# A fused attention and softplus-FFN kernel: loads of q and k in 1 KB packets, w_in in 2 KB packets, a load order planned per tensor, last blocks in free score banks

## Chip, cores, metric

The kernel runs on one core of a Trainium2 chip. The metric is the device time of one execution in microseconds; the profile's span (first to last instruction) is about 1.8 us shorter. Most executions of this kernel agree within about 1%; a run more than 1.5% above the fastest of its kernel counts as slow and is left out of every ratio.

PE is the matrix engine and PEld its weight loads, DVE the vector engine, ACT the scalar engine, POOL the general engine. SyncE (SP in the profile) and ACT issue the loads; SPq and ACTq are their issue queues. "First unit" means the first one or two attention blocks.

## The reference, cut to what matters

```python
# q, k, v: (4, 8, 768, 64) f32; n_global 8, n_local 96; w_in (512, 2048), w_out (2048, 512)
scores = q @ k.T / 8 + bias            # bias = -slope[head] * distance
keep   = (key < 8) | ((0 <= query - key) & (query - key < 96))
a      = softmax(where(keep, scores, -1e9))
x      = (a @ v) as (3072, 512)        # 24 blocks of 128 rows
h      = x @ w_in                      # "first layer"
out    = softplus(h) @ w_out           # "second layer"
```

## The kernel before

The Python file is a small scheduler. Every instruction is declared as an `op` with an engine, an estimated duration, a rank, and the tiles it reads and writes. A planner simulates the engines and the load queues at build time and writes the instructions out in that order. On the chip, each engine then works strictly through its own list.

The settings that the change touches:

```python
FIRST_UNITS = [[0], [1], [2, 3]]       # first block of sequence 0; of 1; of 2 and 3 together
FIRST_LOADS = "u0 u1 u2 i0 i1 i2 i3 i4 i5 i6 i7 o0 u3 o1 ...".split()
ACT_UNITS = 2                          # second halves of units 0 and 1 are issued by ACT
FILLERS = 90                           # idle matmuls that keep PE's clock up at the start
O_KEYS = {(0, 1): ("s", 3), (1, 0): ("s", 2)}   # where second-layer sums are kept; default "o"
```

Every load of a first unit is two halves (64 partitions each, 512-byte runs), the second half issued by ACT for units 0 and 1. w_in comes as eight loads of 256 columns (1 KB runs) behind all three units; POOL casts all of them to bf16.

```python
def load_unit(i, rank, second="SP"):
    for x, which in enumerate("qkv"):
        ... # later units: one 512 KB load
        for y in range(2):
            eng = second if y else "SP"
            def fn(...):
                return dma_on[eng].dma_start(
                    raw_t[slot][64 * y : 64 * y + 64, 0 : P * nh].rearrange("p (h c) -> p h c", h=nh),
                    part.rearrange("h (p r) d -> p h (r d)", r=2))
```

PSUM holds one score tile of four banks and four tiles of one bank each. The second layer accumulates 16 matmuls into `bank(key)`, and DVE copies the sum out.

```python
s_ps = ps.tile([P, 16, P], F32, name="s_ps")     # four banks, ONE tile
x_ps = ps.tile([P, 512], F32, name="x_ps"); o_ps = ps.tile([P, 512], F32, name="o_ps")
def bank(key):
    if key[0] == "s":
        return s_ps[:, 4 * key[1] : 4 * key[1] + 4, :].rearrange("p a b -> p (a b)")
    return {"x": x_ps, "o": o_ps, "h0": h_ps[0], "h1": h_ps[1]}[key[0]][:]
```

The biases of the later blocks (`dist`, `biasA`: two distance tiles and eight products) are built by DVE early and in its gaps: the distances by 5.7 us, five of the products by 11.6 us and the last three from 20.7 to 21.4 us.

The softmax here doesn't subtract the row's maximum and nothing guards it: scores larger than these inputs give would overflow.

## Time and profile before

| | before |
|---|---|
| time, median of 3 | 235.15 us (233.95 to 236.61) |
| span of the profiled run | 232.6 us |
| PE busy | 214.6 us, 92% |
| first first-layer matmul | 21.2 us |
| sixteen slots of eight first-layer matmuls: last weight load | 50.2 us |
| last weight load of the second layer | 228.2 us |

From the page of the kernel before: the span, and the rows by slices of 5.8 us (busy tenths of PE, granted clock in tenths, and GB/s moved by the DMA engines).

```profile
span 232.6 us, 5037 instructions
...
PE   8979889898995998999999999999999999999883
...
PEclk9999999999998899999999999999999999999998
...
GB/s 156 224 235 350 352 305 375 360 253 223 199 270 168 122 93 239 190 187 216 133 166 163 133 135 119 243 131 242 168 188 176 113 73 68 48 45 36 10 93 45
```

PE's row looks full from the start, but the first 20 us are mostly fillers. To see what is useful I counted PE's weight loads in the trace (one per matmul, and none is missing) and multiplied them by pitches read from the timeline: 0.109 us for a first-layer matmul, 0.2165 for a second-layer matmul or a bias seed, 0.03 to 0.055 for the small ones, nothing for a filler. Every kernel has 195.4 us of useful work by this count. "Lost" below means time minus useful work, and it can be read by stretch:

| kernel before | 0 to 60 us | 60 to 100 | 100 to 220 | 220 to end |
|---|---|---|---|---|
| lost, us | 22.9 | 6.6 | 1.9 | 5.9 |

So there are three places to gain: the start, 60 to 100 us, and the end. These windows of the kernel before show the busy time of each engine, the granted clock, the DMA share and GB/s:

```profile
5.00:10.00 5.00, 4.48 (x41) 3.60 (x40) 2.47 (x10) 2.97 (x10) 1.90 (x5) 1.00 1.03 237
10.00:15.00 5.00, 3.52 (x43) 2.48 (x40) 2.68 (x11) 1.85 (x3) 0.53 (x3) 1.00 1.21 220
15.00:20.00 5.00, 4.95 (x64) 4.20 (x65) 4.78 (x12) 1.08 (x2) 4.43 (x7) 1.00 1.12 304
...
60.00:100.00 40.00, 36.16 (x353) 24.46 (x357) 21.19 (x36) 28.81 (x36) 18.78 (x36) 0.96 0.79 187
```

The timelines of the kernel before, first ACT (its issue queue and its first exponential), then PE. Columns: start, duration, engine, line, operation, tiles, count, and in brackets the idle time before it and what ended it.

```profile
3.72 0.60 ACTq L323 DMA_DIRECT2D raw<-in_k_dram  x1
...
8.74 0.60 ACTq L323 DMA_DIRECT2D raw<-in_v_dram  x1
...
11.57 0.60 ACT L581 ACTIVATE pb<-s_ps 128x512 bf16<-128x512 f32 x1 [0.92 <-DVE biasA L793]
```

```profile
10.81 0.40 PE L546 MATMUL s_ps<-qT,kTf 64*128 64x128 bf16 x8
...
21.17 1.05 PE L657 MATMUL h_ps<-XT,w_in_bf 128*128 128x256 bf16 x8
...
220.75 3.61 PE L704 MATMUL o_ps<-w_out_bf,g 128*128 128x512 bf16 x16 [0.78 <-DVE osb L728]
225.15 3.61 PE L704 MATMUL o_ps<-w_out_bf,g 128*128 128x512 bf16 x16 [0.78 <-DVE osb L728]
```

The first scores stand at 10.8 us and the first layer starts at 21.2 us. At the end PE waits twice, 0.78 us each, until DVE has copied the previous block out of the one bank they share.

### The profile page before, as it was taken

How to read it: one execution, taken by the hardware profiler on the slowest of the kernel's cores; microseconds unless marked ns; L12 is line 12 of the kernel's file. 1: busy time of each engine (PE TensorE's matmuls, PEld its weight loads, DVE VectorE, ACT ScalarE, POOL GpSimd, SP SyncE). 2: the span in 40 equal slices, each digit the busy share in tenths (PEclk: the TensorE clock that was granted, in tenths of full speed). 3: DMA queues.
4: the chain of work that ended last, by engine and by line, in shares of the span. 5: the costliest groups of instructions: out<-in, count | busy, mean ns of one | idle time of the engine just before them, and what ended most of it. 6: DMA issues, size and time to landing. Idle time of an engine off the chain costs nothing.

```text
span 232.6 us, 5037 instructions
## 1 busy us (share of the span) xinstructions
PE 214.6 (92%) x1994; PEld 149.0 (64%) x2026; DVE 113.1 (49%) x219; ACT 154.9 (67%) x202; POOL 98.1 (42%) x178
## 2 busy tenths in 40 slices
PE   8979889898995998999999999999999999999883
PEld 5758777555753476777667667676766867667531
DVE  5567315474179494059538448732944862111111
ACT  2432977751985259898878959876885987676600
POOL 3437645789456224767701606341573630000000
PEclk9999999999998899999999999999999999999998
DMA  5999999999796449868877545899679422110021
GB/s 156 224 235 350 352 305 375 360 253 223 199 270 168 122 93 239 190 187 216 133 166 163 133 135 119 243 131 242 168 188 176 113 73 68 48 45 36 10 93 45
DMA packets 76872, 40.97 MB, mean 176 GB/s; under 512 B 30640, under 2 KB 71856, under 8 KB 76848
## 3 DMA queue, kind: packets, MB, share of 16 engines
q1 hardware_dynamic: 75216, 39.86, 68.2%
q10 hardware_dynamic: 1632, 0.79, 1.4%
q8 instruction: 16, 0.26, 0.5%
q14 instruction: 8, 0.07, 0.1%
HBM read 27.26 MB, written 6.29 MB: 144 GB/s over the span
## 4 chain that ended last, share of the span: by engine, by line
PE 78%; DMA 7%; DVE 4%; POOL 3%; issue 3%; ACT 3%; DVEq 0%; POOLq 0%; ACTq 0%
PE o_ps L704 30%; PE h_ps L657 29%; PE s_ps L546 5%; PE h_ps L807 5%; DMA raw<-in_k_dram 4%; PE s_ps L704 3%; DMA raw<-in_v_dram 3%; PE x_ps L601 2%; ACT pb L581 2%; PE x_ps L598 2%; DVE z L572 2%; POOL vb L501 2%; POOL vb L395 1%; DVE osb L728 1%; PE s_ps L443 1%
## 5 line engine op out<-in xcount | busy, mean ns | idle before, releaser
L657 PE MATMUL h_ps<-XT,w_in_bf 128*128 128x256 bf16 x768 | 95.5, 273 | 1.5 <-POOL w_in_bf L350 0.9
L704 PE MATMUL o_ps<-w_out_bf,g 128*128 128x512 bf16 x323 | 84.8, 385 | 4.0 <-DVE osb L728 1.6
L657 PEld LDWEIGHTS <-w_in_bf 128*128 128x128 bf16 x768 | 73.2, 98 | 20.2 <-POOL w_in_bf L350 2.2
L672 ACT ACTIVATE e<-h_ps 128x512 f32<-128x512 f32 x96 | 59.9, 630 | 30.9 <-PE h_ps L657 30.3
L704 PEld LDWEIGHTS <-g 128*128 128x128 bf16 x384 | 35.9, 99 | 36.2 <-issue 7.0
L572 DVE TENSOR_TENSOR z<-s_ps,biasA 128x1024 f32<-128x1024 f32 x40 | 48.1, 1218 | 18.7 <-PE s_ps L546 17.0
L581 ACT ACTIVATE pb<-z 128x1024 bf16<-128x1024 f32 x40 | 41.8, 1050 | 18.9 <-DVE z L572 18.8
L683 ACT ACTIVATE g<-e 128x1024 bf16<-128x1024 f32 x48 | 50.7, 1056 | 1.3
L395 POOL CAST vb<-raw 64x512 bf16<-64x512 f32 (+1 forms) x60 | 32.8, 547 | 23.1 <-DMA raw<-in_v_dram 17.5
L728 DVE COPY osb<-o_ps 128x512 f32<-128x512 f32 (+1 forms) x23 | 15.2, 665 | 51.4 <-PE o_ps L704 51.3
L395 POOL CAST kb<-raw 64x512 bf16<-64x512 f32 (+1 forms) x44 | 24.0, 545 | 17.5 <-DMA raw<-in_k_dram 15.9
L501 POOL COPY vb<-vb 4x512 bf16<-4x512 bf16 x32 | 19.5, 610 | 17.1 <-PE x_ps L601 16.0
L611 DVE TENSOR_TENSOR xs<-x_ps,rcp 128x256 bf16<-128x256 f32 x46 | 19.5, 424 | 1.6
L610 DVE RECIPROCAL rcp<-x_ps 128x4 f32<-128x4 f32 x46 | 8.3, 179 | 22.8 <-PE x_ps L601 19.5
L601 PE MATMUL x_ps<-vb,pb 128*128 128x65 bf16 x160 | 15.1, 194 | 1.6 <-POOL vb L501 1.5
L598 PE MATMUL x_ps<-vb,pb 128*128 128x65 bf16 x160 | 15.5, 194 | 0.7 <-ACT g L683 0.7
L598 PEld LDWEIGHTS <-pb 128*128 128x128 bf16 x160 | 12.5, 98 | 5.2 <-issue 1.9
L492 POOL COPY kT<-kTf 128x32 bf16<-128x32 bf16 x16 | 3.5, 217 | 27.9 <-PE s_ps L546 27.0
L807 PE MATMUL h_ps<-blank 128*128 128x256 bf16 x90 | 13.8, 305 | 1.2 <-POOL blank L751 1.1
L546 PE MATMUL s_ps<-qT,kT 64*128 64x128 bf16 x288 | 13.4, 217 | 0.7 <-DVE z L572 0.7
L601 PEld LDWEIGHTS <-pb 128*128 128x128 bf16 x160 | 11.3, 97 | 3.4 <-issue 1.0
L370 DVE CAST qb<-raw 128x1024 bf16<-128x1024 f32 (+1 forms) x15 | 9.6, 641 | 7.5 <-DMA raw<-in_q_dram 7.5
(49 smaller groups left out, 98.6 us busy)
## 6 DMA issues: line engine op xcount, KB each, us to landing
out_dram<-osb SPq DMA_DIRECT2D x23, 256.0 KB, 2.4
raw<-in_moe_w_in_dram SPq DMA_DIRECT2D x8, 512.0 KB, 9.5
raw<-in_moe_w_out_dram SPq DMA_DIRECT2D x8, 512.0 KB, 8.3
raw<-in_q_dram SPq DMA_DIRECT2D x8, 512.0 KB, 4.3
raw<-in_k_dram SPq DMA_DIRECT2D x8, 512.0 KB, 5.5
raw<-in_v_dram SPq DMA_DIRECT2D x8, 512.0 KB, 4.9
raw<-in_q_dram SPq DMA_DIRECT2D x10, 128.0 KB, 3.5
raw<-in_k_dram SPq DMA_DIRECT2D x10, 128.0 KB, 3.6
```

Of the source, the lines that this page charges most:

```text
L395: copy_on[eng](dst, src[64 * x : 64 * x + 64, r, :, :])
L501: nc.gpsimd.tensor_copy(vb_of(prev)[sl, :, 0:D], vb_of(first)[sl, :, 0:D])
L546: nc.tensor.matmul(s_ps[:, reg, :].rearrange("p (r t) -> p r t", r=2), kt[rows, m, :], qv(rows, m), start=not biased, stop=True, skip_grou ...
L572: nc.vector.tensor_tensor(z[:, 0:nr, :], src, bias, ALU.add)
L581: nc.scalar.activation(pb[:, 0:nr, :], src, AF.Exp, scale=1.0 / root_d)
L598: nc.tensor.matmul(xv[:, m, :], pb[:, 2 * m, :], vb_of(n)[:, h, :], start=True, stop=False)
L601: nc.tensor.matmul(xv[:, m, :], pb[:, 2 * m + 1, :], vb_of(prev)[:, h, :], start=False, stop=True)
L657: last = nc.tensor.matmul(hv[:, j, :], w_in_bf[:, m, fb * P : fb * P + P], XT[g % NXG][:, m, :], start=(m == 0), stop=(m == NM - 1),)
L672: nc.scalar.activation(e[:, p % 2, :, :].rearrange("p j (b t r) -> p (j b) r t", b=2, r=2), hb[:].rearrange("p (a r t) -> p a r t", a=4, r=2),
L683: nc.scalar.activation(gt[:, 2 * p - 2 : 2 * p + 2, :].rearrange("p a t -> p (a t)"), e[:].rearrange("p a j t -> p (a j t)"), AF.Ln, bias=1.0,
L704: nc.tensor.matmul(bank(key), gt[:, fb, ns * P : ns * P + P], w_out_bf[:, fb, :], start=(fb == 0), stop=(fb == NFB - 1),)
L807: nc.tensor.matmul(h_ps[0][:, 0:256], blank[:, 0:P], blank[:])
```

## The change

Its intent: q and k of the first units in 1 KB runs over all 128 partitions; w_in in 2 KB runs; two units of two blocks in place of three units; an order per tensor with w_in tiles in between, found with a planner that also knows that only eight loads can be under way; load leads (how far ahead of its use a unit is loaded) and ranks (its place in the plan) per unit for the middle; and the last four output blocks in the four score banks, with the last half copied and stored by ACT. The diff, cut to its core:

```diff
+    LANES = 8
...
+                        if o.work:
+                            if len(moved) >= self.LANES and not moved[-self.LANES].done:
+                                continue
...
-FIRST_UNITS = [[0], [1], [2, 3]]
-FIRST_LOADS = "u0 u1 u2 i0 i1 i2 i3 i4 i5 i6 i7 o0 u3 o1 o2 o3 o4 o5 o6 o7".split()
+FIRST_UNITS = [[0, 1], [2, 3]]
+FIRST_LOADS = "k0 i1 q0 v0 i4 i5 k1 i7 q1 i0 i3 v1 i2 i6 o0 v2 o1 o2 k2 q2 o4 o5 o6 o7 o3".split()
+ACT_LOADS = "k1 v0 k0".split()
+LEADS = {3: 1.75, 4: 2.5, ...}
+RANK = {0: -4, 1: 0, 2: 8, 3: -12, ...}
-O_KEYS = {(0, 1): ("s", 3), (1, 0): ("s", 2)}
+O_KEYS = {(0, 1): ("s", 3), (1, 0): ("s", 2),
+    (10, 0): ("s", 0), (10, 1): ("s", 1), (11, 0): ("s", 2), (11, 1): ("s", 3)}
+TAIL = 8.0
+ENG = {...}; ENG_X = {...}; ENG_W = {...}     # casts and copies dealt out to DVE, ACT, POOL by hand
...  # load_unit: q and k of a first unit, one block at a time, all partitions
+                                raw[:, c0 : c0 + 256],
+                                src[s_, y::2, sl, :].rearrange("h (p r) d -> p h (r d)", r=4),
...  # load_w: 256 rows x 512 columns in place of 512 rows x 256 columns
+            src = moe_w_in[W * half : W * half + W, 512 * c : 512 * c + 512]
...  # store
+        parts = [(0, 256, "DVE", "SP"), (256, DM, "ACT", "ACT")] if last else [(0, DM, "DVE", "SP")]
...  # biases of the later blocks: only behind the k cast of the second unit
+            if i == len(FIRST_UNITS):
+                late_biases([o for o in pl.ops if o.name == f"castk{len(FIRST_UNITS) - 1}"])
```

Every load of a first unit is now 128 KB (24 of them; before 12 of 128 KB and 6 of 256 KB).

## The prediction

> **What bounds the kernel now.** The span is 232.6 us, PE busy 92% (page). From the timeline of PE: 0.87 us for a slot of 8 first-layer matmuls (L657), 0.2165 us per second-layer matmul (L704). 96 slots, 384 second-layer matmuls, attention and seeds are about 195 us of useful work (my estimate from such pitches). So 38 us are lost, in three places.
>
> 1. Start. The first L657 matmul stands at 21.2 us; before it PE runs mostly fillers (L807). Until 60 us about 26 us are lost. The DMA rows by slices: engines over 90% busy from 5 us on, but 213 to 235 GB/s from 6 to 15 us (q, k, v in 512-byte packets), about 350 from 18 to 28 us (w_in, 1 KB), up to 392 near 35 us (w_out, 2 KB). w_in is issued only after the first three units (from 10.7 us); its casts come 1.5 us apart until 31 us and pace L657.
> 2. Middle. From 60 to 100 us PE idles 3.8 us (windows); there the chain of waits goes through a late v load (64 to 70.7 us) and POOL casts. From 100 to 200 us only 1.7 us.
> 3. End. The last blocks share one bank: twice PE waits 0.78 us for an eviction (L728). The last two half copies run one after the other (0.75 us).
>
> **What the change does.** The Trainium skill ("DMA: Bandwidth & Descriptors", section "Why small descriptors are slow") gives each packet a fixed overhead; the rates above agree in direction. Estimate from them: 2.1 MB of q and k take 6 us instead of 9.3, 4.2 MB of w_in 11.2 instead of 12. v stays slow. So first inputs and w_in are in 4 us earlier. w_in tiles now come between them: the first two slots start at 16 to 19 us. But in the new PE order the value matmuls of the third block stand before the next slots. They need v1, twelfth in the load order: 6.3 MB, so about 23 us, and 2.6 us of POOL casts. So PE waits again until 25 to 26 us. Then all w_in is at hand, and ACT sets the pace: 0.63 + 1.06/2 = 1.16 us per slot against 0.87 on PE. Start: 2.5 us gained (0 to 5), less than the earlier first matmul suggests.
>
> Middle: own load leads per unit and a tuned order should take 2.5 of the 5.5 us idle.
>
> End: four blocks in four score banks remove both 0.78 us waits; the last halves on DVE and ACT with two store queues, 0.35 us. Together 1.9 us.
>
> Added work is small: casts move from POOL to DVE and ACT in the start; key evictions become four copies of 0.3 to 0.4 us.
>
> **Predicted**: 235.15 - 6.9 = 228.2 us, 8 in 10 between 223.5 and 233. Faster by over 2% 0.68, within 2% 0.30, slower 0.02.
>
> **What would show it.** First L657 matmul at 16 to 19 us, then a gap until 25 us ended by v casts; over 300 GB/s from 4 to 12 us; w_out landed some 3 us earlier; under 2 us PE idle from 60 to 100 us; at the end 52 second-layer matmuls without an eviction wait, under 3.6 us from the last matmul to the end.
>
> **What would make it wrong.** Fillers: 39 took 6.57 us, 0.168 each, later ones 0.11; if PE meets inputs late behind 81 of them, the start gains nothing. Many small loads in flight could stall issue. If the reordered middle finds other waits, only the end's 1.9 us remain; if v1 comes earlier than I think, the gain is 9 or more.

## The result and the profile after

The changed kernel takes 246.19 us (median of 4 runs, 245.85 to 246.95); the kernel before took 235.03 us in the runs beside it. The ratio is 1.0474, 95% interval 1.0409 to 1.0539. Ratios here and below are those of fast runs of one kernel against fast runs of the kernel before in the same rounds, so they are not quite the ratio of the medians. The change is a loss of 4.7% where a gain was predicted.

| lost, us | 0 to 60 us | 60 to 100 | 100 to 220 | 220 to end | span |
|---|---|---|---|---|---|
| before | 22.9 | 6.6 | 1.9 | 5.9 | 232.6 |
| changed | 36.4 | 3.9 | 1.5 | 6.9 | 244.2 |
| predicted difference | -2.5 | -2.5 | | -1.9 | |
| measured difference | +13.6 | -2.7 | -0.4 | +1.1 | +11.6 |

(Differences are of unrounded values.) The middle did what was said. The start is 13.6 us worse, the end 1.1 us worse.

The page of the changed kernel, same rows as before; a slice is 6.1 us:

```profile
span 244.2 us, 5065 instructions
...
PE   8825786989889999999999999999999999999873
...
PEclk9995568899999999999999999999999999999998
...
GB/s 136 256 321 222 313 348 341 217 1 164 205 186 186 121 149 258 182 207 214 175 205 191 143 231 266 216 186 195 196 47 47 162 95 43 67 40 3 43 46 86
```

Its windows:

```profile
5.00:10.00 5.00, 4.16 (x41) 3.33 (x39) 1.62 (x4) 0.00 (x0) 1.04 (x1) 1.00 0.86 265
10.00:15.00 5.00, 3.74 (x39) 3.25 (x37) 0.49 (x2) 0.00 (x0) 1.04 (x1) 1.00 1.02 284
15.00:20.00 5.00, 0.00 (x0) 0.00 (x0) 0.36 (x1) 0.00 (x0) 1.04 (x1) 0.74 0.91 268
...
60.00:100.00 40.00, 38.03 (x404) 25.55 (x402) 27.75 (x48) 29.47 (x38) 21.08 (x39) 1.00 0.80 189
```

The loads were not slow: from 5 to 20 us they moved 265, 284 and 268 GB/s against 237, 220 and 304 before, a little more in sum. But from 15 to 20 us PE, PEld and ACT did nothing at all. So the right bytes were missing, not bytes. (The gain in rate that was forecast is missing too: from 4 to 12 us both kernels moved about 240 GB/s.) The chain of waits of the changed kernel says which (start, duration, what):

```profile
5.24 5.49 DMA raw<-in_v_dram
10.75 8.87 DMA raw<-in_v_dram
19.64 0.42 DVE vb L478
...
20.54 0.70 DVE qT L540
...
21.28 0.83 PE s_ps L638 x8
```

It is v of the very first unit. Its second halves are on ACT's queue. ACT's timeline and the waits of SyncE's issue queue ("what waited, for what: total, times, longest") show why they came so late:

```profile
0.74 1.56 ACTq L378 DMA_DIRECT2D raw<-in_k_dram  x2
...
9.13 2.23 ACTq L388 DMA_DIRECT2D raw<-in_v_dram  x2
```

```profile
SPq L378 <- DMA raw<-in_moe_w_in_dram: 3.9, 1, 3.9
```

ACT finished its biases at 4.5 us, but its next issue came at 9.13 us. By the semaphores in the trace, it waited for the load that had used its semaphore before: a half of q that SyncE had issued at 3.30 us and that landed at 9.11 us. The issue of 10.75 us waited in the same way for a half of v that landed at 10.73 us. Later, from 11.4 to 15.3 us, a q load (L378) on SyncE waited 3.9 us for a w_in load with which it shares no data. This is the ring of eight completion semaphores: in the built program, the waits of these loads are on such a semaphore, which frees when the load that used it last has landed. The kernel before has this wait as well (its ACT issue of 8.74 us waits for a load that landed at 8.72 us), but its first scores come only at 10.8 us, so there it cost nothing. With two issuing queues, one queue's issue waits for the other queue's landing, and while it waits nothing else on that engine runs.

DVE then passes the delay on. Its timeline in the changed kernel, and PE's:

```profile
9.08 1.42 DVE L556 COPY kTf<-s_ps 128x256 bf16<-128x256 bf16 x4 [0.72 <-PE s_ps L532]
19.64 0.86 DVE L478 CAST vb<-raw 64x512 bf16<-64x512 f32 x2 [9.15 <-DMA raw<-in_v_dram]
20.54 0.69 DVE L540 COPY qT<-s_ps 128x1024 bf16<-128x1024 bf16 x1
...
38.97 1.10 DVE L877 TENSOR_SCALAR biasA<-dist 128x256 bf16<-128x256 f32 x5
39.99 0.69 DVE L416 CAST w_in_bf<-raw 128x1024 bf16<-128x1024 f32 x1
```

```profile
21.28 0.83 PE L638 MATMUL s_ps<-qT,kTf 64*128 64x128 bf16 x8 [7.54 <-DVE qT L540]
...
32.82 1.46 PE L752 MATMUL h_ps<-XT,w_in_bf 128*128 128x256 bf16 x6
...
40.74 3.09 PE L752 MATMUL h_ps<-XT,w_in_bf 128*128 128x256 bf16 x16 [1.52 <-DVE w_in_bf L416]
...
228.79 3.61 PE L799 MATMUL s_ps<-w_out_bf,g 128*128 128x512 bf16 x16 [0.78 <-DVE osb L824]
233.19 3.61 PE L799 MATMUL s_ps<-w_out_bf,g 128*128 128x512 bf16 x16 [0.78 <-DVE osb L824]
237.58 2.75 PE L799 MATMUL s_ps<-w_out_bf,g 128*128 128x512 bf16 x12 [0.78 <-DVE osb L824]
```

The q copy (L540) was ready but stood behind the v casts in DVE's list, so the scores came at 21.3 us (before 10.8) and the first layer at 32.8 us (before 21.2). A second queue forms on DVE later: the w_in cast of 39.99 us stood behind the biases of the later blocks, though its load had landed at 29.7 us, and PE waited 1.52 us for it. After the idle stretch the granted clock was 0.5 from 17.4 to 34.5 us, and again from 41.3 to 44.7 us. And at the end the eviction wait is not gone: it comes three times now, although each block has a bank of its own.

### The profile page after: what moved, and what is told of

Read it like the earlier page. It is cut to its first block, busy times and chain, and to the rows that moved or that the text cites. A ratio compares the mean times of both kernels' runs of the same rounds, so it can differ in the third digit from the quotient of the medians.

```text
span 244.2 us, 5065 instructions
## 1 busy us (share of the span) xinstructions
PE 221.3 (91%) x2026; PEld 151.7 (62%) x2026; DVE 119.4 (49%) x224; ACT 158.3 (65%) x207; POOL 89.8 (37%) x164
## 4 chain that ended last, share of the span: by engine, by line
PE 80%; DVE 8%; DMA 6%; SPq 2%; ACT 2%; issue 1%; DVEq 0%
PE h_ps L752 33%; PE o_ps L799 25%; PE s_ps L799 9%; DMA raw<-in_v_dram 6%; PE s_ps L638 5%; DVE z L667 2%; PE x_ps L696 2%; PE x_ps L693 2%; DVE osb L824 2%; SPq L378 1%; PE s_ps L532 1%; PE h_ps L901 1%; ACT pb L676 1%; DVE far L861 1%; DVE far L858 1%
## 5 line engine op out<-in xcount | busy, mean ns | idle before, releaser
L752 PE MATMUL h_ps<-XT,w_in_bf 128*128 128x256 bf16 x768 | 98.9, 277 | 1.7 <-DVE w_in_bf L416 1.5
L799 PE MATMUL o_ps<-w_out_bf,g 128*128 128x512 bf16 x288 | 73.9, 380 | 0.5 <-DVE osb L824 0.5
L478 POOL CAST vb<-raw 64x512 bf16<-64x512 f32 (+1 forms) x50 | 27.4, 547 | 14.5 <-DMA raw<-in_v_dram 12.3
L478 POOL CAST kb<-raw 64x512 bf16<-64x512 f32 (+1 forms) x44 | 24.3, 552 | 11.4 <-DMA raw<-in_k_dram 9.6
L824 DVE COPY osb<-o_ps 128x512 f32<-128x512 f32 x18 | 12.4, 690 | 31.1 <-PE o_ps L799 31.1
L799 PE MATMUL s_ps<-w_out_bf,g 128*128 128x512 bf16 x96 | 23.2, 379 | 3.8 <-DVE osb L824 3.1
L593 POOL COPY vb<-vb 4x512 bf16<-4x512 bf16 x32 | 20.0, 625 | 17.1 <-PE x_ps L696 16.0
L705 DVE RECIPROCAL rcp<-x_ps 128x4 f32<-128x4 f32 x45 | 8.1, 180 | 26.0 <-PE x_ps L696 21.3
L676 ACT ACTIVATE pb<-s_ps 128x512 bf16<-128x512 f32 x8 | 4.6, 596 | 22.2 <-PE s_ps L638 20.0
L693 PEld LDWEIGHTS <-pb 128*128 128x128 bf16 x160 | 12.7, 98 | 3.0
L824 DVE COPY osb<-s_ps 128x512 f32<-128x512 f32 (+1 forms) x6 | 3.9, 648 | 21.7 <-PE s_ps L799 21.7
L901 PE MATMUL h_ps<-blank 128*128 128x256 bf16 x90 | 13.1, 308 | 1.1 <-POOL blank L846 1.1
```

The lines of the kernel that those rows point to most:

```text
L478: copy_on[eng](dst, raw)
L593: nc.gpsimd.tensor_copy(vb_of(prev)[sl, :, 0:D], vb_of(first)[sl, :, 0:D])
L676: nc.scalar.activation(pb[:, 0:nr, :], src, AF.Exp, scale=1.0 / root_d)
L693: nc.tensor.matmul(xv[:, m, :], pb[:, 2 * m, :], vb_of(n)[:, h, :], start=True, stop=False)
L752: last = nc.tensor.matmul(hv[:, j, :], w_in_bf[:, m, fb * P : fb * P + P], XT[g % NXG][:, m, :], start=(m == 0), stop=(m == NM - 1),)
L799: nc.tensor.matmul(bank(key), gt[:, fb, ns * P : ns * P + P], w_out_bf[:, fb, :], start=(fb == 0), stop=(fb == NFB - 1),)
```

## The experiments

Theory at first: the start is lost by the late issue of v0 on ACT's queue and by the DVE order behind it; the end by the one tile that holds the four score banks. Rivals: the load order as such (w_in tiles between the inputs), the halved clock, and the packet change.

### Which part of the start: order, clock, DVE list

`a_tail_xo` changes only the end (last four blocks in turn in two separate tiles):

```diff
-    (10, 0): ("s", 0), (10, 1): ("s", 1), (11, 0): ("s", 2), (11, 1): ("s", 3),
+    (10, 1): ("x",), (11, 1): ("x",),     # the others stay in "o"
```

> The changed kernel, but the last blocks go in turn to o_ps and x_ps, which are two tiles, in place of four banks of the one tile s_ps. Theory S (the program orders matmuls and evictions on one tile after another even where the banks differ): the three waits of 0.78 us on L824 near the end go away, 2.3 us faster than the changed kernel (about 244). Rival R (the wait is for something else, a free output slot or the eviction engine itself): the waits stay and so does the time, 246.

Measured: 242.34 us, ratio 1.0242 (1.0172 to 1.0311), against 1.0474. The span fell from 244.2 to 241.0 us, and no second-layer matmul of the last blocks waits for an eviction. From 220 us on, 4.2 us are lost instead of 6.9. So the tile is the cause at the end. (The ratio fell by about 5.5 us' worth, more than the 2.7 us that the end shows. The kernel before was itself about 1 us slower in these rounds, 236.13 against 235.03 us: ratios of different rounds can differ by some tenths of a per cent without a cause in the kernel.)

`a_qfirst` moves the four v0 casts behind the q copy in the emitted order:

```diff
     order = pl.run()
+    late = [o for o in order if o.name.startswith("castv0.")]
+    order = [o for o in order if o not in late]
+    at = next(x for x, o in enumerate(order) if o.name == "cpq0") + 1
+    order[at:at] = late
```

> The changed kernel, only DVE's two pairs of v casts of the first unit stand behind the copy of the transposed q instead of around it. Theory H (PE's 7.5 us hole is head-of-line blocking on DVE: the q copy was ready near 12.7 us and stood behind a cast whose v landed at 19.6 us): first scores near 13 us instead of 21.3, but the value matmuls still need v at 20 us, so the first first-layer matmul comes only 3 to 6 us earlier; 3 to 6 us faster. Rival L (the late v0 load alone decides): scores move but nothing behind them, under 1 us.

Measured: 245.16 us, 1.036 (1.0292 to 1.0429). The scores come at 13.4 us, as early as one could wish, but PE then stands still for the value matmuls instead. PE's timeline of `a_qfirst`:

```profile
13.37 0.83 PE L638 MATMUL s_ps<-qT,kTf 64*128 64x128 bf16 x8
...
21.76 0.38 PE L691 MATMUL x_ps<-vb,pb 128*128 128x65 bf16 x4 [6.48 <-DVE vb L478]
```

The first layer starts at 30.5 instead of 32.8 us. The DVE order costs 1.1% by the ratios (1.0474 to 1.036), whose intervals overlap, and 1.3 us by the loss until 60 us (36.4 to 35.1): less than the 3 to 6 us of theory H. The larger part is that v0 itself is late.

`a_warm` puts 66 more fillers before the first scores, so that PE stays busy while it waits:

```diff
+    base = next(o for o in order if o.name == "fill0")
+    at = next(x for x, o in enumerate(order) if o.name == "sc0")
+    order[at:at] = [base] * 66
```

> The changed kernel with 66 more fillers on PE (7.2 us of matmuls without use) in front of the first scores, in the hole. They delay nothing. Theory C (the halved clock from 17.4 to 34.5 us is a consequence of the hole and costs by itself): clock stays at 1.00 there, 3 to 6 us faster. Rival: PE is then waiting for loads and copies anyway and the clock costs under 1 us.

Measured: 247.49 us, 1.0472 (1.039 to 1.0555), no gain. The granted clock was 1.00 until 36 us, as intended, and the first layer started at 30.0 instead of 32.8 us, but the last weight load of the sixteenth slot came at 66.4 instead of 67.8 us: at 39.3 us PE waited 3.65 us for a w_in cast behind the biases in DVE's list, and the clock was 0.5 from 36.1 to 42.9 us. The Trainium skill ("TensorE: Matmul & The Clock Gate", section "What's actually happening") says that the clock drops to half after an idle window of about 3.4 us. The trace agrees (7.5 us idle, then 0.5 for 17.1 us). Here, though, PE met the late w_in cast anyway, so in this kernel the half clock of the first hole does not set the time, to within some 2 us (the intervals). What it would cost with that cast out of the way, this run does not show.

`a_plain` keeps all of the change except the order of the first loads, and plans anew:

```diff
-FIRST_LOADS = "k0 i1 q0 v0 i4 i5 k1 i7 q1 i0 i3 v1 i2 i6 o0 v2 ..."
+FIRST_LOADS = "k0 q0 v0 k1 q1 v1 i0 i1 i2 i3 i4 i5 i6 i7 o0 k2 q2 v2 o1 ..."
```

> The changed kernel with the packets, engines and middle of the change, but the first loads in plain order: q, k, v of both units, then w_in, then w_out with the next unit between. The plan is made anew. Theory O (the mixed load order starves v0 behind large w_in packets and holds up the queues): v0 lands by 11 us, first first-layer matmul by 21 us, time 230 to 236. Rival P (the small packets spread over all partitions or the wait for DMA lanes is at fault, whatever the order): v0 still lands after 16 us and the time stays over 241.

Measured: 252.55 us median. Three of its four runs, among them the profiled one, were slow and only one (248.09 us) fast, so it has no ratio, and I read its trace only for the order of events. The second halves of v0 were issued no earlier by ACT (9.5 and 10.7 us). The last of them landed at 15.4 instead of 19.6 us, between what the two theories said, so the w_in loads in front seem to cost v0 some 4 us on top of its late issue. The first scores came at 12.6 us, but the k of the second unit, again issued by ACT (13.5 us), was cast only at 19.2 us, and the first layer started at 32.3 us. So the mixed order by itself is not the cause: with the plain order the first layer starts just as late.

### The issuing queue

`a_sponly` is the changed kernel with the very same plan, but all first loads issued by SyncE:

```diff
-   return dma_on[eng].dma_start(     # twice, in load_unit
+   return nc.sync.dma_start(
```

> The changed kernel with the same plan, but all its first loads are issued from SP; none from ACT. Theory Q (the ACT queue's loads are the late ones: their issue waits behind ACT's own work and for DMA lanes, and their landing takes 7 to 9 us): v0 lands near 12 us instead of 19.6, the hole of PE before the first scores shrinks from 7.5 us to under 2, time 4 to 7 us less than the changed kernel. Rival (the sum of bytes in front of v0 decides, whatever queue): v0 lands after 16 us, under 2 us less.

Measured: 237.84 us, 1.0151 (1.0097 to 1.0205): 3.2 of the 4.7 per cent are gone. DVE's timeline of `a_sponly`:

```profile
11.78 1.20 DVE L478 CAST vb<-raw 64x512 bf16<-64x512 f32 x2 [1.43 <-DMA raw<-in_v_dram]
13.01 0.69 DVE L540 COPY qT<-s_ps 128x1024 bf16<-128x1024 bf16 x1
```

The v0 cast starts 7.9 us earlier, and the first layer at 24.4 instead of 32.8 us. Two things change at once: no load waits on ACT any more, and v0's second halves go out before two w_in loads that overtook them in the changed kernel. The Trainium skill ("DMA: Bandwidth & Descriptors", section "Issuing engines are not separate DMA queues") says that loads issued by several engines run on the same 16 DMA engines, and that issuing from several saves only the time of the issue, which is usually small. The trace agrees with the first: rates with one queue and with two are alike (269 against 284 GB/s from 10 to 15 us). It differs on "small": an issue of 128 KB mostly takes 0.55 to 0.65 us here. Whether the second queue saves that time depends on the loads (`p_packets` and `p_sponly` below: 246 against 197 GB/s from 5 to 10 us); in the time of the kernel it cost more than it saved.

### The packets alone

`p_packets` takes the changed code with the old settings (three units, old order, ACT for units 0 and 1, old casts): in effect the kernel before with 1 KB runs for q and k, 2 KB for w_in, the biases of the later blocks built late as in the changed kernel, the third unit in twelve loads of 128 KB, and the new planner and code for copies and stores. `p_nolanes` is the same with `LANES = 999`, so a plan that does not count lanes (loads under way). `p_sponly` is `p_packets` with all loads on SyncE.

```diff
 # p_packets, against the changed kernel
-FIRST_UNITS = [[0, 1], [2, 3]]; ACT_LOADS = "k1 v0 k0".split(); ENG = {...}; RANK = {...}; TAIL = 8.0 ...
+FIRST_UNITS = [[0], [1], [2, 3]]; ACT_LOADS = "q0 k0 v0 q1 k1 v1".split(); ENG = {}; RANK = {}; TAIL = 0.0 ...
 # p_nolanes, against p_packets
-    LANES = 8
+    LANES = 999
 # p_sponly, against p_packets
-   return dma_on[eng].dma_start(
+   return nc.sync.dma_start(
```

> The kernel before in units, load order, engines and ranks, with only the new packets: q and k of the first units in 1 KB packets over 128 partitions, w_in in 2 KB packets (the planner is the changed one). Theory N (packets are not the limit: a load of 128 KB needs 4 us or more to land, eight lanes hold 1 MB in flight, so the 16 engines stand partly idle; the change cuts the third unit's q, k, v into twelve loads instead of six): DMA share under 0.9 from 4 to 14 us, v of the third unit lands after 16 us, first first-layer matmul at 21 to 24 us, time 235 to 240. Rival G (the packets help as meant): over 300 GB/s there, first first-layer matmul by 19 us, time 231 to 234.

> As the run with the new packets alone, but the planner does not count lanes, so ACT issues the second unit's k before its table and biases, as in the kernel before. Theory Q (the 8 us that the new packets alone cost come from one load, the ACT half of the second unit's k, issued at 11.8 us): it is issued by 4.5 us, the second unit's k is cast by 10.5 us instead of 15.4, first first-layer matmul near 21 to 24 us instead of 34, time 234 to 238. Rival N (twelve issues of 0.63 us on SP for the third unit decide): still over 240.

> As the run with the new packets alone, same plan, all first loads issued from SP. Theory Q: no load waits behind ACT's work, second unit's k cast by 11 us, but SP has 24 issues of 0.63 us before w_in, so v of the third unit lands near 19 us: time 236 to 240. Rival N (only the number of issues on SP counts): slower than with two queues, over 243.

Measured: `p_packets` 243.01 us, 1.0365 (1.0302 to 1.0427), with its first layer at 34.5 us, a miss for both theories; `p_nolanes` 242.26 us, 1.036 (1.0239 to 1.0482), a miss, since I expected it near the kernel before (its time is that of rival N, the issues on SyncE, but `p_sponly`, with still more of them, is faster); `p_sponly` 238.22 us, 1.0164 (1.0063 to 1.0265). The ACT timelines of `p_packets` and of `p_nolanes`:

```profile
11.80 0.57 ACTq L350 DMA_DIRECT2D raw<-in_k_dram  x1
13.51 0.64 ACTq L360 DMA_DIRECT2D raw<-in_v_dram  x1
...
15.48 1.09 ACT L648 ACTIVATE pb<-s_ps 128x512 bf16<-128x512 f32 x2
```

```profile
12.65 0.63 ACTq L360 DMA_DIRECT2D raw<-in_v_dram  x1
13.31 1.28 ACT L287 ACT_TABLE_LOAD   x1 [5.96 <-DMA raw<-in_k_dram]
14.60 0.60 ACT L648 ACTIVATE pb<-s_ps 128x512 bf16<-128x512 f32 x1
```

In the kernel before, ACT issued its half of the second unit's k at 3.72 us and of v at 8.74 us, and its first exponential ran at 11.57 us. In `p_packets` these stand at 11.80, 13.51 and 15.48 us. `p_nolanes` brings the k issue back to 3.69 us, but the v issue still waits until 12.65 us, and since the table load and the exponentials stand behind it in ACT's list, they come at 14.60 us all the same. That is why it did not help: any issue that waits on ACT blocks the exponentials. With SyncE alone, the first exponential runs at 11.99 us.

`p_sponly` is still 1.6% slower than the kernel before, with its first layer at 27.4 instead of 21.2 us. Two things are in it, and these runs don't separate them. One is the bias work that the change moved (it is in all three kernels; DVE does it from 22.0 us on in `p_sponly`), of which more below. The other is the issue. SyncE issues twelve loads of 128 KB back to back from 5.95 to 13.66 us in `p_packets`, 0.64 us each, so about 205 GB/s by issue alone. Measured were 214 GB/s from 10 to 15 us with a DMA share of 0.78, against a share of 1.21 in the kernel before; `p_sponly`, where SyncE issues all of them, moved 197 GB/s from 5 to 10 us and 205 from 10 to 15. These twelve loads landed 2.4 to 4.4 us after their issue, most of them faster than the "4 us or more" of the expectation. The wider packets do go through faster per byte: the mean time of a packet on its DMA engine, from the trace's packet records of the first 30 us, was 37 ns for 512 bytes, 53 for 1 KB and 90 for 2 KB in the kernel before. This includes waits under load: in `p_packets` it was 30, 56 and 92 ns. An estimate from that: 128 KB in 1 KB packets is eight packets on each of 16 engines, 0.42 us of transfer, less than its 0.64 us of issue. So while the loads are 128 KB, the issue and not the packet sets their rate. The Trainium skill ("DMA: Bandwidth & Descriptors", section "Rules for kernel authors") points the same way: it wants large loads over 128 partitions. No run has 1 KB packets in loads of 256 KB, so packets and load size are not taken apart.

### The end by itself

`b_tail_s` gives the kernel before the end of the changed one; `b_tail_xo` gives it the two separate tiles.

```diff
 # b_tail_s
-O_KEYS = {(0, 1): ("s", 3), (1, 0): ("s", 2)}
+O_KEYS = {(0, 1): ("s", 3), (1, 0): ("s", 2), (10, 0): ("s", 0), (10, 1): ("s", 1), (11, 0): ("s", 2), (11, 1): ("s", 3)}
+TAIL = 8.0
 # b_tail_xo
-O_KEYS = {(0, 1): ("s", 3), (1, 0): ("s", 2)}
+O_KEYS = {(0, 1): ("s", 3), (1, 0): ("s", 2), (10, 1): ("x",), (11, 1): ("x",)}
```

> The kernel before with only the end of the change: the last four blocks in four banks of s_ps and the last group's first layer drawn forward. Theory S (one tile is ordered as one, its banks are not free of each other): PE waits 0.78 us three times in place of twice, time the same or up to 1 us more. Rival (free banks work as meant): no wait, 1.5 us less.

> The kernel before with its last blocks in turn in o_ps and x_ps, two tiles. Theory S: both waits of 0.78 us go, 1.5 us less than before. Rival R (another cause of the wait): no change.

Measured: `b_tail_s` 235.82 us, 1.0036 (0.9944 to 1.0128); `b_tail_xo` 235.42 us over all runs, of which two were slow, and 0.9928 (0.986 to 0.9997) by its two fast ones. One of the three waiting groups at the end of `b_tail_s` (the others stand at 222.37 and 226.76 us), then the last two groups of `b_tail_xo`:

```profile
217.97 3.61 PE L705 MATMUL s_ps<-w_out_bf,g 128*128 128x512 bf16 x15 [0.78 <-DVE osb L729]
```

```profile
220.84 3.62 PE L704 MATMUL o_ps<-w_out_bf,g 128*128 128x512 bf16 x16
224.29 3.62 PE L704 MATMUL x_ps<-w_out_bf,g 128*128 128x512 bf16 x16
```

Four banks of one tile keep the wait; two tiles remove it. The Trainium skill ("PSUM — Partial Sum Buffer", section "Summary: rules for kernel authors") advises to read one bank while matmuls write a different one, and the banks were different here. The wait is one that the program itself holds: its matmuls on `s_ps` wait for the copy out of `s_ps`, whichever bank either of them uses.

### w_in in 2 KB runs, the middle, and combinations on the kernel before

`b_win` is the kernel before with w_in in 2 KB runs. `b_mid` is `b_tail_xo` with the changed kernel's leads, ranks and TAIL. `b_win_xo` is `b_win` with the two tiles at the end; `b_win_mid` is `b_mid` with w_in in 2 KB runs.

```diff
 # b_win
-  raw_t[slot][:].rearrange("p (m c) -> p m c", m=NM), moe_w_in[:, W * p : W * p + W] ...
+  raw_t[slot][:].rearrange("p (a c) -> p a c", a=2), moe_w_in[W * (p % 2) : W * (p % 2) + W, 512 * (p // 2) : ...]
 # b_mid
+LEADS = {4: 1.75, 5: 2.5, ...}; RANK = {0: -4, ...}; TAIL = 8.0      # as in the changed kernel
```

> The kernel before with only w_in in 2 KB packets (halves of 256 rows by 512 columns; its order and all else as before). Theory: packets are no limit in w_in either, since its casts on POOL take 1.04 us each and two halves are now needed for a slot; first first-layer matmul 0.5 to 1.5 us later, then faster; time within 1 us of before. Rival (the packets help as meant): 1 to 2 us less.

> The kernel before with the change's own load leads and ranks of the middle and the ends in turn in o_ps and x_ps; the start is untouched. If the parts add up as read from the traces (2.7 us of the loss between 60 and 100 us, 1.5 us at the end): 230 to 232. If the leads and ranks only fit the changed kernel's start: 234 to 236.

> The kernel before with w_in in 2 KB packets and the last blocks in turn in o_ps and x_ps. If both single gains add up (1.0 and 0.7 per cent): 230 to 232. If the gain of w_in was the new plan's luck between 60 and 100 us, it may be lost again: 233 to 235.

> The same with the change's leads and ranks of the middle. If these add 1 us: 229 to 231. If the new plan spoils the middle: over 232.

| kernel | median us | ratio (95%) | lost 0 to 60 | 60 to 100 | 100 to 220 | 220 to end |
|---|---|---|---|---|---|---|
| before (as above) | 235.15 | | 22.9 | 6.6 | 1.9 | 5.9 |
| b_win | 231.95 | 0.9899 (0.9796 to 1.0001) | 23.0 | 3.0 | 4.5 | 5.2 |
| b_mid | 231.80 | 0.9864 (0.9741 to 0.9987) | 22.9 | 3.1 | 6.0 | 4.3 |
| b_win_xo | 229.35 | 0.9756 (0.9678 to 0.9833) | 22.5 | 2.8 | 2.1 | 4.3 |
| b_win_mid | 231.35 | 0.9808 (0.9729 to 0.9887) | 22.5 | 1.9 | 7.6 | 4.2 |

The profile of `b_mid` fell in a run judged slow, so its row is only a hint. `b_win` missed its theory (within 1 us of before) and gained 2.4 us by the ratio, whose interval just reaches 1; the profile of `b_win_mid` is that of its slowest run. The wider w_in packets bring the casts from 1.49 to 1.36 us apart, but nothing is gained until 60 us. What `b_win` gains lies between 60 and 100 us, where the new plan happens to avoid the stalls of the old one. The leads and ranks move loss out of 60 to 100 us in `b_mid` and `b_win_mid`, and some of it returns after 100 us. So it seems that in this kernel a plan that differs slightly loses 2 to 4 us more or less in one stretch by itself, and a gain of that size in the middle can't be credited to one setting. `b_win_xo` beats both kernels.

### What SyncE alone leaves, and a repaired version

`a_plain_sp` is `a_plain` with SyncE alone. `a_best` is the changed kernel with SyncE alone, the q copy first, and the two tiles at the end.

> The changed kernel with q, k, v of both units before w_in and all first loads issued from SP. Theory O2 (once the second queue is out of the way, the mixed order is the rest): second unit's k cast by 13 us and v by 18 us (18.6 and 27.3 with the mixed order), loss until 60 us 3 us or more below the 29.7 of the mixed order on SP. Rival U (the large first unit and its 24 issues of 0.6 us are the rest): the loss until 60 us stays within 1.5 us of 29.7.

> The changed kernel with three mends at once: first loads on SP alone, q copy ahead of the v casts on DVE, last blocks in turn in o_ps and x_ps. If they add up (7.5, about 1 with v early, and 3 us): 233 to 235, at or just below the kernel before. If they overlap: 236 to 238.

Measured: `a_plain_sp` 246.71 us, 1.0427 (1.0313 to 1.0541), first layer at 25.4 us; it lost 31.9 us until 60 us and 7.4 us from 100 to 220, so the plain order is no better (theory O2 is out; the loss is also outside rival U's range), and its new plan is worse later. `a_best` 236.40 us, 1.0021 (0.9932 to 1.0111): no better than the kernel before. It still loses 30.2 us until 60 us, 7.3 more than before. The chain of waits of `a_sponly` in that stretch names something else:

```profile
29.27 2.36 DVE biasA L877 x5
31.63 0.61 DVE w_in_bf L416
32.28 3.09 PE h_ps L752 x16
```

The biases of the later blocks, which the change moved behind the second unit's k, keep DVE from 26.4 to 31.6 us, and a w_in cast stands behind them. `a_sp_bias` is `a_sponly` with this work early in DVE's list again; `a_best_bias` the same on `a_best`.

```diff
     order = pl.run()
+    late_d = [o for o in order if o.name.startswith(("ddl", "dl1e"))]
+    late_b = [o for o in order if o.name.startswith("biasTrue")]
+    order = [o for o in order if o not in late_d and o not in late_b]
+    at = max(x for x, o in enumerate(order) if o.name.startswith("biasFalse") and o.eng == "DVE") + 1
+    order[at:at] = late_d
+    at = next(x for x, o in enumerate(order) if o.name == "castk0") + 1
+    order[at:at] = late_b
```

> The changed kernel with all first loads on SyncE, plus: the eight biases of the later blocks and their distances stand early in the DVE order (before and behind the first k cast), as in the kernel before, not behind the k casts of the second unit. Theory L (part of the 6.8 us that the SyncE-only kernel still loses until 60 us against the kernel before is the late-bias work: its chain of waits has 5.2 us of it on DVE, 26.4 to 31.6 us, in front of a w_in cast, and PE idles 1.23 + 1.47 us there): the w_in cast that stood at 31.55 us starts at 24 to 28 us, the PE hole at 32.28 us goes, 1.5 to 2.7 us less are lost until 60 us, ratio to the kernel before 1.003 to 1.009 in place of 1.0151. Rival (the loads set that stretch): the cast moves but the matmuls then wait for another w_in tile or for ACT, under 0.5 us gained, ratio 1.013 or more; or the early DVE work delays the first unit's casts and the first scores come over 0.5 us later than 13.96 us.

> The best changed kernel so far (SyncE only, q copy first, last blocks in turn in two tiles) plus the same early biases. Theory L: 1.5 to 2.7 us below its 1.0021, so 0.991 to 0.996. Rival: 1.000 or more.

Measured: `a_sp_bias` 235.61 us, 1.0012 (0.9954 to 1.007); `a_best_bias` 232.00 us, 0.9845 (0.9791 to 0.9899). Both gained somewhat more than expected. DVE's timeline of `a_sp_bias`:

```profile
30.18 0.69 DVE L416 CAST w_in_bf<-raw 128x1024 bf16<-128x1024 f32 x1 [4.39 <-DMA raw<-in_moe_w_in_dram]
```

The cast did not move as far forward as I had expected (30.2 us, not 24 to 28), because now its load ends the wait. But from 30 to 40 us only 0.6 us are lost instead of 3.5, and until 60 us 27.8 instead of 29.7, though the first scores come 0.5 us later. A part of this is the clock: in `a_sponly` it was 0.5 from 32.9 to 36.3 us, behind the hole (the sixteen matmuls of 32.28 us took 3.09 us), while in `a_sp_bias` it stays at 1.00 there and sixteen take 1.92 us.

| changed kernel with | ratio to before | lost until 60 us |
|---|---|---|
| nothing more | 1.0474 | 36.4 |
| q copy first | 1.036 | 35.1 |
| SyncE alone | 1.0151 | 29.7 |
| SyncE alone, early biases | 1.0012 | 27.8 |
| SyncE alone, q copy first, two tiles at the end | 1.0021 | 30.2 |
| all four | 0.9845 | 27.3 |

The four repairs together turn a loss of 4.7% into a gain of 1.6%, without touching the packets, the units or the planned load order. About 4.4 us are still lost more until 60 us than before (27.3 against 22.9). They fit the 24 issues of 0.6 us (the first exponential runs at 14.8 us in `a_sponly` against 11.6 before), but no run isolates this.

## Why the prediction was wrong, point by point

- **Start, predicted 2.5 us gained, measured 13.6 us lost.** The step that failed is "first inputs and w_in are in 4 us earlier" with the estimate from bytes and packet rates ("2.1 MB of q and k take 6 us instead of 9.3"). It failed twice. The rate did not rise: "2.1 MB in 6 us" is 350 GB/s, measured were 240 from 4 to 12 us (237 before) and 265 to 284 in the windows from 5 to 20 us; the last w_in load landed at 31.1 us (30.3 before). And the larger loss came from the path: what was missed is that a load must first be issued. The first unit's v was issued by ACT at 9.1 and 10.8 us because its turn in the ring of eight completion semaphores had not come; it was cast at 19.6 us. I took v1, the twelfth in the order, as the one that PE would wait for until 25 us; it was v0, the fourth. `a_sponly` (1.0474 to 1.0151) shows this, `a_qfirst` the share of the DVE list, and `a_sp_bias` (1.0151 to 1.0012) the share of the bias work that the change moved. The clock as the main cause is ruled out by `a_warm` to within 2 us, the mixed order by itself by `a_plain` and `a_plain_sp`, as far as their poorer later plans allow.
- **"The first two slots start at 16 to 19 us"**: 32.8 us. "w_out landed some 3 us earlier" was wrong too: its first load landed at 32.5 us against 31.8 before.
- **"Added work is small"** was the second error: "casts move from POOL to DVE and ACT" was counted as work, not as places in DVE's list. What hurt was not their duration: the q copy waited behind a v cast, and a w_in cast behind the biases.
- **Middle, predicted 2.5 us gained with under 2 us of PE idle from 60 to 100 us**: right. PE idled 1.97 us there (40 minus 38.03) instead of 3.84, and 2.7 us less were lost; the granted clock rose too, from 0.96 to 1.00 (it was 0.5 for 3.4 us in the kernel before). The runs on the kernel before show that such a gain also comes with other plans, so that it came out right is in part luck.
- **End, predicted 1.9 us gained, measured 1.1 us lost.** The step that failed is "four blocks in four score banks remove both 0.78 us waits". There were 52 second-layer matmuls at the end as said, but with three such waits, since the banks belong to one tile. `a_tail_xo`, `b_tail_s` and `b_tail_xo` show it. The last halves stayed in series as well: ACT's copy started at 240.83 us, after DVE's of 240.37 us, and from the last matmul to the end it took 3.9 us (3.8 before), not under 3.6.
- **What could make it wrong** named the right thing ("Many small loads in flight could stall issue") but the chance of slower was put at 2%. The wait lists of the built program, which need no chip, hold the wait of ACT's v0 issue on another load's semaphore, so they should have shown it; this was not tried.

## What to carry to other kernels

Count issues before bytes: a load costs its issue time (here some 0.6 us), and its turn among the completion semaphores (here 4.6 us on ACT), before it costs bandwidth, and an issue that has to wait must not sit on an engine whose next instruction the critical path needs. When engines run fixed lists, any reordering puts something behind something else, so look for what now stands behind the least certain arrival, and move ready work, such as the q copy and the biases, ahead of it. Free memory is free only in the unit in which the program tracks it, here the tile and not the bank.

## What the Trainium skill lacked or had wrong

- "DMA: Bandwidth & Descriptors", section "Issuing engines are not separate DMA queues": it calls the issue time usually small. Here a 128 KB load mostly took 0.55 to 0.65 us to issue, about 0.42 us to transfer in 1 KB packets (estimate from 53 ns a packet), and rows of such loads held the stream at 197 to 214 GB/s. (Against the 2.4 us and more from issue to landing it is small.)
- The same section lacks the case in which a second issuing engine costs time: with completion semaphores used in turn, ACT's issues came 4.6 us after ACT was free (4.5 to 9.1 us), and moving the issues to SyncE took the ratio from 1.0474 to 1.0151.
- "DMA: Bandwidth & Descriptors", section "Why small descriptors are slow (HBM only)": it gives a fixed overhead of about 3 cycles per packet on top of one cycle for 32 bytes. By that, a byte in 512-byte packets would cost 1.13 times as much as in 2 KB packets (19/16 against 67/64; my estimate from that page, without the descriptor bytes that it names as a second cost). In the kernel before, a packet took 37 ns with 512 bytes, 53 with 1 KB and 90 with 2 KB, waits under load included, so 1.6 times (37 against 90/4); in `p_packets`, with less load on the engines during the 512-byte packets, 1.3 times (30 against 92/4). How much of either is the overhead, these runs do not show.
- "TensorE: Matmul & The Clock Gate" has the drop to half clock right (7.5 us idle, then 0.5 for 17.1 us). It lacks that such a stretch may cost nothing where something later ends last: keeping the clock at 1.00 until 36 us changed the ratio from 1.0474 to 1.0472, since PE then waited 3.65 us for a cast.
- No page has that a PSUM tile of four banks is ordered as one: 0.78 us for each block at the end, gone with separate one-bank tiles. This is the program's dependency tracking and not the chip.
